# Second layer's first block in seven products, and a token job in every tick

## The chip, the core and the metric

The kernel runs on one core of one Trainium2 chip. The time is device microseconds of a run, first to last instruction with what the launch adds; smaller is better. TensorE is called PE below, VectorE DVE, ScalarE ACT, GpSimd POOL, and SyncE, which issues the DMAs, SP.

## The reference

An attention over 4 batches of 8 heads, with 512 local and 32 global positions of 64 columns, gives 4 x 544 = 2176 tokens of 512 columns. Two gated layers follow; their shapes are 512 x 1536 for gate and value and 1536 x 512 for the output:

```python
def _moe_ref(x, w_gate, w_val, w_out, rms_g):
    xn = x / np.sqrt(np.mean(x * x, -1, keepdims=True) + 1e-06) * rms_g
    g = xn @ w_gate
    silu = g * (1.0 / (1.0 + np.exp(-g)))
    val = xn @ w_val
    return silu * val @ w_out

def _moe2_ref(x, w_gate, w_val, w_out):
    gate = 1.0 / (1.0 + np.exp(-(x @ w_gate)))
    val = x @ w_val
    return gate * val @ w_out
```

The second layer reads the first layer's output. Weights and tokens come as numbers wider than 16 bits and the result is held close to fp32, so that each is split into a high and a low fp16 part, and a product of two such is three matmuls (high by high, low by high, high by low).

## The kernel before

The two layers are cut into twelve blocks of 256 hidden columns, 0 to 5 of the first layer and 6 to 11 of the second. The tokens lie as columns in three parts q = 0, 1, 2 of 768, 768 and 640 tokens; `HN[q]` is half of a part: 384, 384, 320 columns. (6,0) below is block 6 on part 0.

**Products.** Blocks 0 to 2 and, before the change, block 6 (`GP = 6`) are multiplied in the plain way. Block 6 does it in `plain_gv` (L462): for each of two row halves of the weights, two halves of the part, and gate and value, 12 matmuls into one PSUM bank: 96 matmuls of `HN[q]` columns for a part. The other blocks use `quad_gv`: gate and value are each a 2 x 2 by 2 x 2 block product, done with seven products for eight; a product (`prod`, L364) is 6 matmuls, so 84 matmuls for a part. It needs sums of the weights' four pieces and sums of the tokens' four pieces. Its products go to PSUM in four pairs for the gate and four for the value, the first pair holding only one product; the pool `pp` has four buffers of one pair each, used in turn and shared with the output products. ACT copies the first product out (`sa`, L428); DVE adds the other pairs into the tiles G and V (L421: four adds for each, of 2, 2, 1 and 2 products). Then ACT applies the gate (L407), DVE multiplies (L397), ACT writes the high fp16 part `h` (L398) and POOL the low one (L401).

**Weights.** `w_block(g)` queues the steps that convert a block's three matrices, `w_step` takes one off. A conversion is ACT's L139 on each half of the raw words, DVE's L151 and L154 (step 1) and L157 (step 2). For gate and value of a block in seven products come sums: POOL L249 and L250, then DVE L254 and L255; ACT writes high parts (L187) and DVE low parts (L190), of the four pieces (128x1024) and of the three sums (128x768). A plain block has no sums. `w_need(g, 0)` in front of a block runs all steps that are still missing.

**Token sums.** When a part of the first layer's output `yacc[q]` is done, `y_combos(q)` queues jobs that write its fp16 parts `xhi` (ACT L627) and `xlo` (DVE or POOL L630) and then the sums: L590 in place on `yacc` (two on DVE, one on POOL, for each `kt`), then the parts `tt` of the sums (ACT L596, POOL L599). `quad_gv` reads `tt` and three of the four quarters of a part's `xhi` and `xlo`; `plain_gv` reads all four quarters and no `tt`. `j_need(q, i)` runs the jobs of a part that are still missing; before a plain block only those of `xhi` and `xlo`.

**Order.** All of it is written out by hand: every product and output piece calls `tick`, and a tick takes a token job every `pace[2]` ticks and a weight step every `pace[1]`. Engines run their instructions in that order. `GROUPS` pairs blocks for the output products: (4,0), (4,1), (5,0), (4,2), (5,1), (5,2), then (6,0), (6,1), (7,0), (6,2), (7,1), (7,2). The outputs of a part (`out1`, L499, of the first layer; `out2`, L521, of the second; eviction L481 on DVE or L479 on ACT) are issued behind the next block's products: those of part 0 of blocks 4 and 5 behind (4,2), of part 1 behind (5,2), of part 2 behind (6,0).

Of the kernel before, what the change touches and what calls it, by code (L numbers as in the profile page):

```python
# [12 lines left out]
AF = mybir.ActivationFunctionType  # L13
ALU = mybir.AluOpType
# [5 lines left out]
def tile_attention_moe_moe(  # L20
# [17 lines left out]
    nc = tc.nc  # L38
# [33 lines left out]
    xhi = [res.tile([128, 4, 128 * n], F16, tag=f"xhi{i}", name=f"xhi{i}") for i, n in enumerate(PT)]  # L72
    xlo = [res.tile([128, 4, 128 * n], F16, tag=f"xlo{i}", name=f"xlo{i}") for i, n in enumerate(PT)]
# [15 lines left out]

    GS = 3  # L90

    GP = 6
    raw_t = []

    w_pos = [0, 0]
# [35 lines left out]
    def w_scale(n):  # L131

        if n >= NPC or not wide:
            return
        words = w_words.setdefault(n, [])
        if len(words) < 2:
            f = f_tile(n)[:, len(words)]
            words.append(raw_t.pop(0))
            nc.scalar.activation(out=f, in_=words[-1][:, :, 1].bitcast(F32), func=AF.Copy, scale=2.0 ** -112)  # L139
# [57 lines left out]
    def w_block(g):  # L197
# [7 lines left out]
        def small(f):  # L205

            def f2():
                f()
                w_step()
            return f2  # L210
# [5 lines left out]
        def conv(w):  # L216
            n = 3 * g + w
            if g < GS:
                return [lambda: (late(), w_half(n, 0)), lambda: w_half(n, 1)]
            return [lambda: (late(), w_conv1(n)), lambda: w_conv2(n)]  # L220
# [17 lines left out]
        else:  # L238
# [21 lines left out]
            def lo(w, i):  # L260
                a, b = (0, 4)[i], (4, 7)[i]
                w_lo(box[w][i], w_t[g][0][:, w, 0, a:b], w_t[g][0][:, w, 1, a:b])
                if i == 0:
                    w_f.pop(3 * g + w)

            for w in range(2):
                jobs += conv(w)
                if g == GP:
                    def parts(w=w):
                        return [w_t[g][0][:, w, a, 0:4].rearrange("p (j a) f -> p j (a f)", j=2) for a in range(2)]  # L270
                    jobs.append(plain(w, parts))
                else:
                    jobs += [lambda w=w: sums(w), lambda w=w: (sums2(w), hi(w, 0)), lambda w=w: (lo(w, 0), hi(w, 1)),
                             lambda w=w: (lo(w, 1), w_scale(3 * g + w + 1))]
            if g == GP:
                jobs.append(small(late))
# [17 lines left out]
    def w_need(g, i):  # L294
        while not w_done[g][i]:
            w_step()
# [248 lines left out]
    def j_need(q, i):  # L545
        while any(x[0] == q and x[1] <= i for x, _ in jobs):
            jobs.pop(0)[1]()
# [32 lines left out]
    EG = [nc.vector if c == "d" else nc.gpsimd for c in "ddpppppdpd"]  # L580

    def combos(q, kt, b):


        def f(i):
            x = b()

            o, i0, i1 = ((x[:, 0], x[:, :, 1], x[:, 0]), (x[:, 1, 1], x[:, 1, 1], x[:, 0, 0]),
                         (x[:, 1, 0], x[:, 1, 0], x[:, 1, 1]))[i]
            EG[i].tensor_tensor(out=o, in0=i0, in1=i1, op=ALU.subtract)  # L590

        def part(a):
            return tt_t[q][:, a, :, kt].rearrange("p (u v) n -> p u v n", u=2)

        def f2(u):
            nc.scalar.activation(out=part(0)[:, u], in_=b()[:, u], func=AF.Copy)  # L596

        def f3(u):
            EG[4 + u].tensor_tensor(out=part(1)[:, u], in0=b()[:, u], in1=part(0)[:, u], op=ALU.subtract)  # L599
        jobs.extend(((q, 1), x) for x in (lambda: f(0), lambda: (f(1), f2(0)), lambda: (f(2), f3(0)),  # L600
                                     lambda: f2(1), lambda: f3(1)))

    def tt_alloc(q):
        tt_t[q] = pb[1].tile([128, 2, 4, 2, HN[q]], F16, tag=f"tt{q}", name=f"tt{q}")
# [17 lines left out]
    def y_combos(q):  # L622
        n = HN[q]
        yd = yacc[q].rearrange("p (d n) -> p d n", d=4)

        def f(k):
            nc.scalar.activation(out=xhi[q][:, k], in_=yd[:, k], func=AF.Copy)  # L627

        def f2(k):
            EG[8 + k % 2].tensor_tensor(out=xlo[q][:, k], in0=yd[:, k], in1=xhi[q][:, k], op=ALU.subtract)  # L630

        jobs.append(((q, 0), lambda: (tt_alloc(q) if q not in tt_t else None, f(0))))
        jobs.extend(((q, 0), lambda k=k: (f(k), f2(k - 1))) for k in range(1, 4))
        jobs.append(((q, 0), lambda: f2(3)))
        for kt in range(2):
            combos(q, kt, lambda kt=kt: yd[:, kt:4:2].rearrange("p u (t n) -> p u t n", t=2))
# [470 lines left out]
    pace = [0, 2, 2]  # L1107
# [22 lines left out]
    with tc.manual_schedule():  # L1130
# [33 lines left out]
        def flush():  # L1164

            while pend:
                g, key = pend.pop(0)
                if g == group[g][-1]:
                    outs(g, key)
                if 0 < g < GS and key in (2, chunks_b[-1], last.get(g)):  # L1170
                    w_block(g + 2)
                    pace[1] = [2, 4, 3, 3, 4, 4, 4, 2, 4, 2, 2, 2][g]
                if g == NBLK - 1:
                    if isinstance(key, int):
                        y_combos(key)
                    elif key[1] > 0:
                        y_combos(key[0])
# [29 lines left out]
        st_ps.close()  # L1207
        pb["ps"] = st_ps.enter_context(tc.tile_pool(name="pp", bufs=4, space=PSUM, reuse_waits="tile"))
        pb[2] = st_p2.enter_context(tc.tile_pool(name="pb2", bufs=1, reuse_waits="tile"))
        pace[2] = 3  # L1210
        for gr in GROUPS[GS:]:
            a, b = gr[0], gr[-1]
            for g, q in [(a, q) for q in range(3)] if a == b else [(a, 0), (a, 1), (b, 0), (a, 2), (b, 1), (b, 2)]:
                w_need(g, 0)
                j_need(q, 0 if g == GP else 1)
                (plain_gv if g == GP else quad_gv)(g, q, flush)
                if q == 2 and g + 2 < 2 * NBLK:
# [39 lines left out]
```

## Time and profile before

| | |
|---|---|
| median of 3 runs | 938.59 us (936.45 to 938.75) |
| profiled execution, its own time | 939.76 us |
| its span | 938.0 us |
| PE busy | 884.8 us, 94% |
| DVE busy | 666.7 us, 71% |
| ACT, POOL busy | 368.6 and 345.6 us |
| mean granted clock of PE | 0.975 |

The span is cut by the page into 40 slices with the busy share of each engine and PE's granted clock in tenths. The chain of waits follows the work back from the last instruction and names what each step stood behind. Timelines list an engine's instructions in order, equal neighbours merged, with the idle time before them and what ended it. A matmul's row is longer than its turn on PE, since matmuls overlap: the turn is the distance between starts.

### The profile page before, as it was taken

The page shows a single profiled execution, that of the slowest core. Times are in us where ns is not written, and L with a number is a line of the kernel's source. Part 1 is how long each engine was busy: PE and PEld are TensorE (multiplying, and loading weights), DVE is VectorE, ACT ScalarE, POOL GpSimd, SP SyncE. Part 2 cuts the span into 40 slices and gives each one's busy share as a digit, 9 for nine tenths or more (in the row PEclk, how much of TensorE's full clock was granted, in tenths as well). Part 3 has the DMA queues.
Part 4 walks back from the last instruction along what each step waited for, and adds up shares of the span by engine and source line. Part 5 has one row for each costly group of instructions (what it writes and reads, how often), then busy time and mean ns, then how long its engine had stood idle before and what let it go on. Part 6 is the DMA issues. An engine that isn't in the chain of part 4 may idle for free.

```text
span 938.0 us, 19228 instructions
## 1 busy us (share of the span) xinstructions
PE 884.8 (94%) x8119; PEld 551.6 (59%) x8119; DVE 666.7 (71%) x935; ACT 368.6 (39%) x685; POOL 345.6 (37%) x396
## 2 busy tenths in 40 slices
PE   7667889999996999999999799999999999999998
PEld 4455556666674666666666466656556655556553
DVE  3887786646468687899966967737598557997352
ACT  3665565445353343333333344433344213333120
POOL 5548656564354772222221263242221303022120
PEclk9789899999999999999999899999999999999999
DMA  9764452210012111121201121101122011200102
GB/s 194 179 141 102 91 140 53 55 26 2 5 42 95 45 45 46 46 90 45 74 19 45 45 89 46 45 1 46 45 90 90 1 45 45 90 23 1 68 23 101
DMA packets 88999, 58.13 MB, mean 62 GB/s; under 512 B 58448, under 2 KB 83536, under 8 KB 88912
## 3 DMA queue, kind: packets, MB, share of 16 engines
q1 hardware_dynamic: 88912, 56.90, 21.9%
q8 instruction: 64, 1.05, 0.5%
q14 instruction: 23, 0.19, 0.1%
HBM read 52.17 MB, written 4.46 MB: 60 GB/s over the span
## 4 chain that ended last, share of the span: by engine, by line
PE 77%; DVE 14%; issue 3%; ACT 2%; DMA 2%; POOL 1%; SPq 0%; DVEq 0%; ACTq 0%; POOLq 0%
PE p L364 28%; PE p L521 13%; PE b L311 11%; PE p L499 7%; PE b L499 6%; PE p L462 5%; PE b L740 3%; DVE wf L154 2%; DVE wf L157 2%; DVE wf L151 2%; PE b L864 1%; PE b L809 1%; DVE x L854 1%; DVE G L421 1%; DVE wc L190 1%
## 5 line engine op out<-in xcount | busy, mean ns | idle before, releaser
L364 PEld LDWEIGHTS <-wc 128*128 128x128 f16 x2016 | 198.2, 98 | 122.3 <-DVE G L421 4.8
L364 PE MATMUL p<-tt,wc 128*128 128x384 f16 (+1 forms) x1152 | 202.4, 319 | 5.9 <-DVE G L421 5.4
L401 POOL TENSOR_TENSOR h<-V,h 128x768 f16<-128x768 f32 (+1 forms) x48 | 80.8, 1704 | 236.0 <-ACT h L398 218.8
L364 PE MATMUL p<-xhi,wc 128*128 128x384 f16 (+1 forms) x576 | 157.0, 318 | 0.5 <-DVE ya L481 0.5
L311 PE MATMUL b<-xhi,wgv 128*128 128x384 f16 (+1 forms) x576 | 144.0, 320 | 0.0
L521 PE MATMUL p<-wo,h 128*128 128x512 f16 x612 | 133.4, 379 | 0.0
L499 PEld LDWEIGHTS <-wo 128*128 128x128 f16 x864 | 84.7, 99 | 57.1 <-issue 10.2
L311 PEld LDWEIGHTS <-wgv 128*128 128x128 f16 x864 | 83.2, 98 | 47.2 <-issue 3.4
L521 PEld LDWEIGHTS <-h 128*128 128x128 f16 x612 | 59.9, 98 | 71.0 <-POOL h L401 0.2
L311 PE MATMUL b<-xlo,wgv 128*128 128x384 f16 (+1 forms) x288 | 92.1, 320 | 1.3 <-DVE xlo L914 1.3
L364 PE MATMUL p<-xlo,wc 128*128 128x384 f16 (+1 forms) x288 | 91.6, 318 | 0.0
L481 DVE SCALAR_TENSOR_TENSOR ya<-p,ya 128x768 f32<-128x768 f32 (+3 forms) x42 | 42.3, 1016 | 62.1 <-PE p L521 48.2
L697 POOL COPY vw<-vt 32x520 f32<-32x520 f32 (+1 forms) x92 | 80.9, 880 | 12.0 <-DMA vt<-in_v_l_dram 7.8
L499 PE MATMUL b<-hhi,wo 128*128 128x384 f16 (+1 forms) x288 | 73.4, 322 | 8.1 <-ACT hhi L342 7.4
L428 ACT ACTIVATE sa<-p 128x384 f32<-128x384 f32 (+1 forms) x48 | 22.5, 469 | 133.6 <-PE p L364 120.8
L343 POOL TENSOR_TENSOR hlo<-t,hhi 128x384 f16<-128x384 f32 (+1 forms) x36 | 38.4, 1066 | 90.5 <-ACT hhi L342 90.4
L398 ACT ACTIVATE h<-V 128x1536 f16<-128x1536 f32 (+1 forms) x24 | 33.9, 1413 | 95.2 <-DVE V L397 95.2
L499 PE MATMUL p<-h,wo 128*128 128x384 f16 (+1 forms) x432 | 67.3, 317 | 0.0
L421 DVE TENSOR_TENSOR V<-p,V 128x768 f32<-128x768 f32 (+3 forms) x72 | 56.6, 786 | 12.4 <-PE p L364 9.6
L421 DVE TENSOR_TENSOR G<-p,G 128x768 f32<-128x768 f32 (+3 forms) x72 | 56.5, 785 | 8.4 <-PE p L364 5.9
L154 DVE SCALAR_TENSOR_TENSOR wf<-raw,wf 128x512 int32<-128x512 int32 x72 | 55.8, 806 | 1.6
L157 DVE SCALAR_TENSOR_TENSOR wf<-raw,wf 128x512 int32<-128x512 int32 x72 | 53.9, 778 | 0.6
(137 smaller groups left out, 1320.4 us busy)
## 6 DMA issues: line engine op xcount, KB each, us to landing
raw<-in_moe_w_gate_dram SPq DMA_DIRECT2D x24, 512.0 KB, 3.7
raw<-in_moe_w_val_dram SPq DMA_DIRECT2D x24, 512.0 KB, 4.4
raw<-in_moe_w_out_dram SPq DMA_DIRECT2D x24, 512.0 KB, 3.9
k<-in_k_l_dram SPq DMA_DIRECT2D x16, 256.0 KB, 4.0
q<-in_q_l_dram SPq DMA_DIRECT2D x16, 256.0 KB, 4.2
vt<-in_v_l_dram SPq DMA_DIRECT2D x32, 128.0 KB, 4.8
out_dram<-ya SPq DMA_DIRECT2D x16, 256.0 KB, 2.2
vg<-in_v_g_dram SPq DMA_DIRECT2D x16, 64.0 KB, 3.7
```

The lines of the kernel that those rows point to most:

```text
L154: nc.vector.scalar_tensor_tensor(out=u[:, j], in0=w_words[n][j][:, :, 1], scalar=-0x80000000, in1=u[:, j], op0=ALU.bitwise_and, op1=ALU.bi ...
L157: nc.vector.scalar_tensor_tensor(out=u[:, j], in0=w_words[n][j][:, :, 0], scalar=29, in1=u[:, j], op0=ALU.logical_shift_right, op1=ALU.bit ...
L311: nc.tensor.matmul(p[:, 0:n], wgv[:, j, gv, a, k * 128:(k + 1) * 128], x[xi][:, k, o:o + n], start=(i == 0), stop=(i == 11),)
L343: EH[3].tensor_tensor(out=lo, in0=t, in1=hi, op=ALU.subtract)
L364: nc.tensor.matmul(p, wc[:, w, a, wi, kt * 128:(kt + 1) * 128], r, start=(i == 0), stop=(i == 5))
L401: EH[j // 2].tensor_tensor(out=lo[:, i:i + 2], in0=vj[:, i - j:i - j + 2], in1=hi[:, i:i + 2], op=ALU.subtract)
L421: nc.vector.tensor_tensor(out=o, in0=p, in1=i, op=ALU.add)
L462: nc.tensor.matmul(gv[:, w], wc[:, w, a, c, (k % 2) * 128:(k % 2 + 1) * 128], x[q][:, k, h * n:(h + 1) * n], start=(i == 0), stop=(i == 11))
L481: nc.vector.scalar_tensor_tensor(out=ya, in0=p, scalar=1.0 / WS, in1=ya, op0=ALU.mult, op1=ALU.add)
L499: nc.tensor.matmul(p[:, i, 0:n], wo[:, j, a, d * 128:(d + 1) * 128], hh[:, j, ho:ho + n], start=(c == 0), stop=(c == 6 * len(gr) - 1),)
L521: nc.tensor.matmul(p[:, i], hh[:, j, (i0 + i) * 128:(i0 + i + 1) * 128], wo[:, j, a, :], start=(c == 0 and g == gr[0]), stop=(c == 5 and g ...
L697: eng.tensor_copy(out=dst, in_=src)
```

## The change

`GP` becomes `None`: no block is plain any more, so block 6 goes through `quad_gv`, its weight steps get the sums, and `j_need` asks for its token sums too. `pace[2]` becomes 1: after the first layer's plain blocks a token job is taken in every tick instead of every third. `y_combos` writes only the first half of quarters k = 0 and 1 of `xhi` and `xlo`; the second half of those is read by no product of seven.

```diff
-    GP = 6
+    GP = None
...
+        m = [n, n, 2 * n, 2 * n]
+
         def f(k):
-            nc.scalar.activation(out=xhi[q][:, k], in_=yd[:, k], func=AF.Copy)
+            nc.scalar.activation(out=xhi[q][:, k, 0:m[k]], in_=yd[:, k, 0:m[k]], func=AF.Copy)
 
         def f2(k):
-            EG[8 + k % 2].tensor_tensor(out=xlo[q][:, k], in0=yd[:, k], in1=xhi[q][:, k], op=ALU.subtract)
+            EG[8 + k % 2].tensor_tensor(out=xlo[q][:, k, 0:m[k]], in0=yd[:, k, 0:m[k]], in1=xhi[q][:, k, 0:m[k]],
+                                        op=ALU.subtract)
...
-        pace[2] = 3
+        pace[2] = 1
```

Lines behind L626 stand up to four lines later in the changed kernel (`xlo` is L630 before and L633 after).

DVE's instructions at the change from (5,1) to (5,2): in the first row V and G are multiplied for (5,1), L421 adds for (5,2), L590 are token sums of part 0, L157 and L190 convert weights.

```order
 L397 SCALAR_TENSOR_TENSOR V<-V,G 128x1536
 L421 TENSOR_TENSOR G<-p,sa 128x2x320
-L590 TENSOR_TENSOR ya_79<-ya_79 128x768
-L157 SCALAR_TENSOR_TENSOR wf<-raw,wf 128x512 x2
+L190 SCALAR_TENSOR_TENSOR wc<-wf,wc 128x1024
 L421 TENSOR_TENSOR G<-p,G 128x2x320
 L421 TENSOR_TENSOR G<-p,G 128x320
-L590 TENSOR_TENSOR ya_79<-ya_79 128x384
-L421 TENSOR_TENSOR G<-p,G 128x2x320
+L421 TENSOR_TENSOR G<-p,G 128x2x320
+L190 SCALAR_TENSOR_TENSOR wc<-sm,wc 128x768
```

The token sums and the conversion's second step have left this place (they stand in (5,1), ahead of it, or behind the products); a low part of block 6's weights stands there instead.

DVE's instructions before, where (6,1) ends and (7,0) begins (rows with L471 and L473 are the plain block's gate times value and its low part; the last row is the first add of (7,0)):

```order
L190 SCALAR_TENSOR_TENSOR wc<-wf,wc 128x1024
L471 SCALAR_TENSOR_TENSOR G<-p,G 128x384
L473 TENSOR_TENSOR h_7357<-G,h_7356 128x384
L190 SCALAR_TENSOR_TENSOR wc<-sm,wc 128x768
L471 SCALAR_TENSOR_TENSOR V<-p,V 128x384
L473 TENSOR_TENSOR h_7357<-V,h_7356 128x384
L151 TENSOR_SCALAR wf<-wf 128x1024
L154 SCALAR_TENSOR_TENSOR wf<-raw,wf 128x512 x2
L590 TENSOR_TENSOR ya_80<-ya_80 128x768
L157 SCALAR_TENSOR_TENSOR wf<-raw,wf 128x512 x2
L421 TENSOR_TENSOR G<-p,sa 128x768
```

The same place now; the first row is the last add of (6,1), the last the first add of (7,0):

```order
L421 TENSOR_TENSOR V<-p,V 128x768
L254 TENSOR_TENSOR sm<-wf 128x256
L255 TENSOR_TENSOR sm<-wf,sm 128x256
L190 SCALAR_TENSOR_TENSOR wc<-wf,wc 128x1024
L190 SCALAR_TENSOR_TENSOR wc<-sm,wc 128x768
L151 TENSOR_SCALAR wf<-wf 128x1024
L154 SCALAR_TENSOR_TENSOR wf<-raw,wf 128x512 x2
L397 SCALAR_TENSOR_TENSOR V<-V,G 128x1536
L157 SCALAR_TENSOR_TENSOR wf<-raw,wf 128x512 x2
L421 TENSOR_TENSOR G<-p,sa 128x768
```

Between the last add of one block and the first of the next there are now eight rows in one piece, the steps that `w_need(7, 0)` ran at once among them.

POOL's instructions from the start of (6,0) until block 7's gate sums, now:

```order
L633 TENSOR_TENSOR xlo_77<-ya_80,xhi_74 128x384
L633 TENSOR_TENSOR xlo_77<-ya_80,xhi_74 128x768
L590 TENSOR_TENSOR ya_80<-ya_80 128x384
L599 TENSOR_TENSOR tt_4738<-ya_80,tt_4738 128x2x384 x2
L590 TENSOR_TENSOR ya_80<-ya_80 128x384
L599 TENSOR_TENSOR tt_4738<-ya_80,tt_4738 128x2x384
L401 TENSOR_TENSOR h_7084<-V,h_7083 128x768 x2
L599 TENSOR_TENSOR tt_4738<-ya_80,tt_4738 128x2x384
L249 TENSOR_TENSOR sm<-wf 128x256
L250 TENSOR_TENSOR wf<-wf 128x256
```

Before, only the two L630 rows of part 1, one late L599 of part 0 and the sums L249 and L250 stood in this stretch; the four L599 of part 1 stood in (6,1) and (7,0), and there was no L401 of block 6.

## Rows read from the trace of the kernel before

**Rows 1.** Waits of PE from 360 us on: total us, times, longest.

```profile
PE p L364 <- DVE G L421: 5.4, 3, 4.4
```

**Rows 2.** PE's timeline, (5,2) and the outputs behind it: start, us, instruction [idle before].

```profile
521.55 0.97 PE L364 MATMUL p<-tt,wc 128*128 128x320 f16 x6 [0.59 <-DVE G L421]
...
527.77 3.38 PE L364 MATMUL p<-tt,wc 128*128 128x320 f16 x12 [4.43 <-DVE G L421]
...
533.68 15.76 PE L499 MATMUL p<-h,wo 128*128 128x384 f16 x96
```

**Rows 3.** DVE's timeline around that wait.

```profile
521.42 0.95 DVE L590 TENSOR_TENSOR ya<-ya 128x768 f32<-128x768 f32 x1
522.28 4.17 DVE L157 SCALAR_TENSOR_TENSOR wf<-raw,wf 128x512 int32<-128x512 int32 x2
526.38 1.33 DVE L421 TENSOR_TENSOR G<-p,G 128x640 f32<-128x640 f32 x2
527.63 0.55 DVE L590 TENSOR_TENSOR ya<-ya 128x384 f32<-128x384 f32 x1
528.10 0.82 DVE L421 TENSOR_TENSOR G<-p,G 128x640 f32<-128x640 f32 x1
...
529.56 2.38 DVE L190 SCALAR_TENSOR_TENSOR wc<-wf,wc 128x1024 f16<-128x1024 f32 x1
```

**Rows 4.** POOL's timeline there.

```profile
522.14 3.77 POOL L401 TENSOR_TENSOR h<-V,h 128x768 f16<-128x768 f32 x2 [8.84 <-ACT h L398]
...
529.22 1.65 POOL L599 TENSOR_TENSOR tt<-ya,tt 128x768 f16<-128x768 f32 x1
```

**Rows 5.** Stretches: us; busy (count) PE, PEld, DVE, ACT, POOL; PE's clock; DMA.

```profile
501.70:538.80 37.10, 32.08 (x195) 19.86 (x194) 34.10 (x41) 15.86 (x20) 10.09 (x6) 0.91 0.17 57
549.30:607.20 57.90, 57.90 (x374) 36.41 (x373) 44.11 (x60) 26.56 (x41) 19.80 (x15) 1.00 0.17 55
```

**Rows 6.** Two earlier idle times of PE in its timeline.

```profile
288.63 0.32 PE L499 MATMUL b<-hhi,wo 128*128 128x384 f16 x1 [3.06 <-ACT hhi L342]
...
304.18 0.27 PE L499 MATMUL b<-hhi,wo 128*128 128x256 f16 x1 [4.31 <-ACT hhi L342]
```

**Rows 7.** Stretches, columns as above: PE's clock behind each of three idle times.

```profile
290.00:292.00 2.00, 2.00 (x14) 1.21 (x13) 2.00 (x2) 1.20 (x3) 2.00 (x2) 1.00 0.25 87
...
306.00:308.00 2.00, 2.00 (x11) 1.40 (x10) 0.58 (x2) 1.12 (x2) 2.00 (x2) 0.52 0.00 0
...
528.00:530.00 2.00, 2.00 (x9) 1.18 (x8) 2.00 (x4) 1.76 (x3) 1.74 (x2) 0.50 0.70 228
```

**Rows 8.** Chain of waits in order of time: start, us, engine, line, count.

```profile
570.28 23.40 PE p L462 x144
593.68 13.65 PE p L364 x84
```

**Rows 9.** DVE's timeline in an earlier block in seven products.

```profile
454.22 0.41 DVE L254 TENSOR_TENSOR sm<-wf 128x256 f32<-128x256 f32 x1
...
455.01 0.95 DVE L421 TENSOR_TENSOR G<-p,G 128x768 f32<-128x768 f32 x1
455.88 1.22 DVE L190 SCALAR_TENSOR_TENSOR wc<-wf,wc 128x1024 f16<-128x1024 f32 x1
457.01 0.95 DVE L421 TENSOR_TENSOR V<-p,sa 128x768 f32<-128x768 f32 x1
...
461.42 0.68 DVE L151 TENSOR_SCALAR wf<-wf 128x1024 int32<-128x1024 int32 x1
462.13 1.29 DVE L154 SCALAR_TENSOR_TENSOR wf<-raw,wf 128x512 int32<-128x512 int32 x2
463.35 1.75 DVE L397 SCALAR_TENSOR_TENSOR V<-V,G 128x1536 f32<-128x1536 f32 x1
465.01 1.30 DVE L157 SCALAR_TENSOR_TENSOR wf<-raw,wf 128x512 int32<-128x512 int32 x2
466.22 0.96 DVE L421 TENSOR_TENSOR G<-p,sa 128x768 f32<-128x768 f32 x1
```

## The prediction

> **What bounds the kernel now.** I first read PE's waits behind the attention [rows 1]: the reader is to see that from 360 us on PE waits almost only for DVE's adds into G, 5.4 us in three times, 4.4 of them in one. So in this half PE sets the time, and DVE decides where PE stands still. PE's timeline puts the long wait into (5,2), right ahead of the changed block [rows 2]: 0.59 and 4.43 us, and then 24 matmuls of 320 columns that take from 527.77 to 533.68. The stretches show why: at 528 to 530 us the granted clock is 0.50, the lower level (1.2 GHz) [rows 7]. DVE is busy for 34.10 of 37.10 us there, but for 44.11 of 57.90 in (6,0) to (7,0), where PE never waits [rows 5].
>
> DVE's and POOL's timelines, laid side by side, give the price that matters [rows 3, 4]. The two L157 need 1.2 us elsewhere (465.01 to 466.22 [rows 9]); at 522.28, while POOL runs two L401 from 522.14 to 525.91, they take 4.17. L190 at 529.56 takes 2.38 for 1.22, beside L599. The adds L421 at 526.38 and 528.10, whose one input is in PSUM, keep their time. DVE thus lost 3.0 + 1.2 = about 4.1 us to 10.09 us of POOL work [rows 5], a share of 0.41. I call this the lock.
>
> **Step 1, the products.** Plain: 144 matmuls of 384 columns in 23.40 us, so 15.60 for 96; in sevens 84 take 13.65 [rows 8]. Two parts save 1.95 each, the part of 320 columns 1.63 by its columns: 5.5 us off PE, which is full there.
>
> **Step 2, (5,1) and (5,2).** The order shows block 6's conversions thinned out (its sums come in between) and part 0's token sums pulled ahead of them. DVE's work from 501.70 to the third add of (5,2)'s G, by distances between starts [rows 3, 9]: conversion 1.93 and 1.21, `xlo` 0.47 + 0.86, the adds of (5,1) 6.5 (0.87 for two products, 1.25 x 384/320 = 1.5 for two and one; both twice, for G and V, with another 0.87), token sums 2 x (0.86 + 0.47), L254 and L255 0.79, L397 1.66, first add of (5,2) 0.73 by its columns, low part 1.13, adds 1.25: 19.2 us. POOL's work beside it, 1.65 us per 768 columns [rows 4], is 5504 columns, 11.8 us; at 0.41 the lock costs 4.8. The add ends at 525.7. PE would want it at 527.77 - 4.43 - 0.59 = 522.7, so it waits 3.0 us for 5.0, in pieces, since the adds are late one by one. An idle time of 3.06 us left the clock at 1.00, those of 4.31 and 4.43 were followed by 0.52 and 0.50 [rows 6, 7, 2]; so the fall goes too. It cost 5.9 us for matmuls of 3.25 (24 x 13.65/84 x 320/384): 2.7. Step 2 gains 5.0 - 3.0 + 2.7 = 4.7, call it 4.8 with the half quarters of `xlo`. Without any lock it would be 7.7, with twice the lock a loss of 2.6 (7.6 us of waits, and the clock falls).
>
> **Step 3, (6,0) to (7,0).** Here the plain block's cover goes. PE from the start of (6,0) to where it needs the first add of (7,0): 14 products 13.65, outputs of part 2 13.0 (96 x 0.1355), 14 products 13.65, then eight of (7,0) 7.8, since four PSUM pairs let PE run ahead of an add by five products: 48.1 us. DVE has to do until that add ends: adds 6.5 + 6.5 + 0.87 = 13.9; five L481 3.8; part 1's and 2's `xlo` and token sums 4.0 + 3.4; two L397 3.3; and for the weights four conversions of 3.14, three low parts of 1.13 and three of 0.86, sums 2 x 0.79, 20.2: together 48.6. That alone is PE's whole time, and POOL's work comes on top: `xlo`, L590, L599, L401 and two pairs of sums, 11072 columns, 23.8 us, at 0.41 a lock of 9.8. Before, most of it had 14 us of free DVE time beside it [rows 5]. DVE also waits for POOL, for L250 behind two L401 and an L599, about 1 us. 48.6 + 9.8 + 1 - 48.1 = 11.3 us of waits of PE. Bounds: no more lock than the 4.1 us measured gives 4.6 (no wait for POOL); a share of 0.6, 15.8. I take 0.41, measured where DVE was as full.
>
> The Trainium skill, page "SBUF — State Buffer", section "Who interferes with whom", says that a DVE instruction with two SBUF inputs and a GpSimd instruction that reads SBUF exclude each other for whole instructions, and that one with a single SBUF input is free. The trace agrees in L157's 4.17 us and the adds' unchanged time. By that rule POOL's 23.8 us lie free only beside the 17.7 us of adds and evictions, so the lock is at least 6.1, the waits at least 7.6 and the time at least 938.6; by the rows it is what follows.
>
> **Step 4, the clock there.** The waits grow toward (7,0): between the last add of (6,1) and the first of (7,0) stand L254, L255, two L190, a conversion and L397, 8 us of DVE work in one piece, where PE's lead is five products, 4.9 us, and is already used up. So I expect a last wait of over 4 us and a fall of the clock like that at 528 us: 2.7.
>
> **What costs nothing.** ACT's halved L627 and its table load, which moves from L470 to L407, lie on an engine that DVE does not wait for there. The sums' ACT work goes behind POOL's. SP's DMAs stand as before. The new wait of DVE in (5,1), L254 for L250, holds one add, which PE wants 4 us later; uncovered it costs 1. `j_need` finds its jobs done. Behind (7,0) the conversions shift by a row or two, where waits of 0.4 to 0.5 us are all there is: plus or minus 1.
>
> **The sum.** The profiled execution took 939.76, 1.2 over the median; the differences belong to either, and I put them on the median: 938.6 - 5.5 - 4.8 + 11.3 + 2.7 = 942.3.
>
> **Rivals.** First: the same waits, but in pieces too short for the clock to fall: 939.6. For it, 3.06 us left the clock up; against it, the eight rows in one piece. Second, faster: DVE keeps up. Mechanism: POOL's work meets DVE's gaps and adds, not its two-input work, in (6,0) and (6,1), so that the lock stays at 4.1 and the first add of (7,0) ends within 53 us of the start of (6,0). Waits 4.6, no fall: 938.6 - 5.5 - 4.8 + 4.6 = 932.9. For it: from 549 to 607 us POOL worked 19.80 us without a wait of PE; against it: DVE was then busy for three quarters and would now be full. Third, worse: POOL's and DVE's instructions alternate and each holds the other, share 0.6: waits 15.8, time 946.8. For it: L157's second instruction stood behind a second L401.
>
> **How the numbers follow.** Forecast 0.42, no fall 0.20, DVE keeps up 0.22, worse 0.16. The forecast alone is 939.5 to 945 (step 2's waits 2 us either way, the lock 1 to 2). 0.3% is 2.8 us and about what a measurement of this kernel tells from no change: faster means below 935.8, slower above 941.4. The forecast falls slower with 0.25 and same with 0.17; no fall gives same 0.15, faster 0.03, slower 0.02; the second rival faster 0.18, same 0.04; the third is slower. Together faster 0.21, same 0.36, slower 0.43. Leaving out a tenth at each end, from the second rival's lower half and the third's upper, the range is 932.3 to 947.
>
> **What would show it.** Step 1: no L462 and 84 matmuls of (6,0) in 13.7 us where it doesn't wait. Step 2: the waits in (5,2) under 4 us, clock 1.00 in the 20 us behind, and the outputs of part 1 starting near 529 for 533.7. Step 3: PE's waits for L421 from (6,0) to (7,0) of 9 to 13 us, the longest at (7,0); DVE full there, with L157, L190, L397 and `xlo` above their usual time. Step 4: a stretch at 0.5 behind it. If those waits are under 6 us, step 3 is wrong and the lock is not additive; if the waits in (5,2) are as long as before, step 2 is.

## The result and the profile after

The changed kernel took 948.04 us (median of 4 runs, 946.88 to 948.44), the kernel before, run beside it, 938.67 (936.45 to 938.98). The ratio is 1.0108, 95% interval 1.0096 to 1.0120. The change costs 9.4 us. The forecast was 942.3 with a range up to 947.0: the direction was right, the loss more than twice what the sum gave, and the time lies above the range.

The waits of PE behind the attention, of after; the columns are those of [rows 1]:

```profile
PE p L364 <- DVE V L421: 8.8, 5, 2.5
PE p L364 <- DVE G L421: 6.5, 5, 4.7
PE p L364 <- POOL tt L599: 3.0, 1, 3.0
PE p L364 <- ACT sa L428: 1.1, 1, 1.1
PE p L364 <- DVE ya L481: 0.5, 1, 0.5
```

The reader is to see two things: the waits of 5.4 us in three times have become 19.9 in 13, and two of them are not for DVE: a short one for ACT, and one of 3.0 us for POOL, which no step of the prediction had. The timeline of PE tells where they lie, first those of (5,1) and (5,2), which answer to [rows 2]:

```profile
516.21 1.80 PE L364 MATMUL p<-tt,wc 128*128 128x320 f16 x12 [1.43 <-DVE V L421]
520.01 0.30 PE L364 MATMUL p<-xhi,wc 128*128 128x320 f16 x1 [2.00 <-DVE V L421]
523.22 0.97 PE L364 MATMUL p<-tt,wc 128*128 128x320 f16 x6 [0.60 <-DVE G L421]
525.61 1.80 PE L364 MATMUL p<-tt,wc 128*128 128x320 f16 x12 [0.61 <-DVE G L421]
528.88 15.76 PE L499 MATMUL p<-h,wo 128*128 128x384 f16 x96
```

and then the two longest ones from (6,0) to (7,0):

```profile
576.65 0.80 PE L364 MATMUL p<-tt,wc 128*128 128x384 f16 x2 [2.95 <-POOL tt L599]
...
609.14 2.08 PE L364 MATMUL p<-tt,wc 128*128 128x384 f16 x6 [4.74 <-DVE G L421]
```

With 0.22, 2.24, 2.48 and 1.12 us beside them they make 13.75 us. The clock behind both, in the stretches of after, columns as in [rows 7]:

```profile
576.00:578.00 2.00, 1.35 (x5) 0.66 (x5) 0.00 (x0) 0.00 (x0) 1.92 (x3) 0.53 0.03 8
578.00:580.00 2.00, 2.00 (x10) 0.94 (x9) 1.85 (x4) 1.89 (x3) 0.08 (x1) 0.62 0.00 0
...
608.00:610.00 2.00, 0.85 (x3) 0.41 (x3) 1.90 (x3) 2.00 (x3) 1.39 (x1) 0.50 0.49 138
610.00:612.00 2.00, 2.00 (x8) 0.93 (x7) 1.86 (x4) 0.56 (x2) 1.86 (x2) 0.50 1.05 369
```

The spans of the two profiled executions differ by 8.6 us (946.6 and 938.0), and the starts of (5,1), (6,0) and (7,1) in PE's timelines, first of before, then of after, divide this into pieces:

```profile
500.63 0.33 PE L364 MATMUL p<-xhi,wc 128*128 128x384 f16 x1
549.28 0.33 PE L462 MATMUL p<-xhi,wc 128*128 128x384 f16 x1
635.75 0.33 PE L364 MATMUL p<-xhi,wc 128*128 128x384 f16 x1
...
498.52 0.33 PE L364 MATMUL p<-xhi,wc 128*128 128x384 f16 x1
544.48 0.33 PE L364 MATMUL p<-xhi,wc 128*128 128x384 f16 x1
644.15 0.33 PE L364 MATMUL p<-xhi,wc 128*128 128x384 f16 x1
```

Up to the start of (5,1), 498.52 for 500.63, the two kernels issue the same work; the 2.1 us belong to the executions (in the eleven traces here with the same work up to that point it starts between 496.85 and 500.63). From there to the outputs of part 1 (called the first stretch from here on) it is 30.36 us for 33.05, a gain of 2.7. From the start of (6,0) to that of (7,1) (the second stretch) it is 99.67 for 86.47, a loss of 13.2. The outputs between the two take the same time in both, and behind (7,1) the difference is 0.2. So the whole loss lies in the second stretch, and there the products save their 5.5 us while PE stands still for 13.75 and loses about 5.0 more, most of it by being slowed twice.

What DVE did in that stretch, its timeline of after, eight pieces of it:

```profile
548.36 2.73 DVE L157 SCALAR_TENSOR_TENSOR wf<-raw,wf 128x512 int32<-128x512 int32 x2
...
559.23 3.45 DVE L590 TENSOR_TENSOR ya<-ya 128x768 f32<-128x768 f32 x2
...
564.06 1.85 DVE L151 TENSOR_SCALAR wf<-wf 128x1024 int32<-128x1024 int32 x1
...
578.12 0.42 DVE L254 TENSOR_TENSOR sm<-wf 128x256 f32<-128x256 f32 x1 [4.74 <-POOL wf L250]
...
589.00 3.57 DVE L154 SCALAR_TENSOR_TENSOR wf<-raw,wf 128x512 int32<-128x512 int32 x2
...
594.62 1.95 DVE L157 SCALAR_TENSOR_TENSOR wf<-raw,wf 128x512 int32<-128x512 int32 x2
...
599.35 1.61 DVE L254 TENSOR_TENSOR sm<-wf 128x256 f32<-128x256 f32 x1 [0.26 <-POOL wf L250]
...
608.14 0.95 DVE L421 TENSOR_TENSOR G<-p,sa 128x768 f32<-128x768 f32 x1
```

and POOL's timeline beside its idle time:

```profile
571.57 3.44 POOL L401 TENSOR_TENSOR h<-V,h 128x768 f16<-128x768 f32 x2 [6.20 <-ACT h L398]
574.97 1.63 POOL L599 TENSOR_TENSOR tt<-ya,tt 128x768 f16<-128x768 f32 x1
576.56 0.71 POOL L249 TENSOR_TENSOR sm<-wf 128x256 f32<-128x256 f32 x1
577.36 0.72 POOL L250 TENSOR_TENSOR wf<-wf 128x256 f32<-128x256 f32 x1
```

Two L401, an L599 and the weights' first sums stand on POOL in one row. PE waits for the L599 until 576.6, DVE for the L250 until 578.1, with an L481 and all that follows queued behind it. The first add of (7,0) starts at 608.14, the eight rows ahead of it come in one piece from 599.35, as the order had shown.

### The profile page after: what moved, and what is told of

The parts are those of the page before. It is cut to its first block, busy times and chain, and to the rows that moved or that the text cites. A ratio compares the mean times of both kernels' runs of the same rounds, so it can differ in the third digit from the quotient of the medians.

```text
span 946.6 us, 19184 instructions
## 1 busy us (share of the span) xinstructions
PE 882.5 (93%) x8083; PEld 546.5 (58%) x8083; DVE 684.4 (72%) x944; ACT 368.4 (39%) x675; POOL 355.4 (38%) x406
## 4 chain that ended last, share of the span: by engine, by line
PE 72%; DVE 18%; issue 3%; ACT 2%; POOL 2%; DMA 1%; SPq 1%; DVEq 0%; ACTq 0%; POOLq 0%
PE p L364 30%; PE p L521 14%; PE b L311 11%; PE b L499 6%; PE p L499 6%; DVE wf L154 3%; PE b L744 2%; DVE wf L151 2%; DVE wf L157 2%; DVE G L421 1%; PE b L868 1%; DVE ya L590 1%; DVE x L858 1%; POOL vw L701 1%; DVE V L421 1%
## 5 line engine op out<-in xcount | busy, mean ns | idle before, releaser
L364 PEld LDWEIGHTS <-wc 128*128 128x128 f16 x2268 | 222.4, 98 | 153.4 <-issue 21.7
L364 PE MATMUL p<-tt,wc 128*128 128x384 f16 (+1 forms) x1296 | 227.6, 319 | 16.3 <-DVE V L421 6.8
L401 POOL TENSOR_TENSOR h<-V,h 128x768 f16<-128x768 f32 (+1 forms) x54 | 90.0, 1687 | 259.1 <-ACT h L398 224.8
L364 PE MATMUL p<-xhi,wc 128*128 128x384 f16 (+1 forms) x648 | 177.3, 320 | 3.6 <-DVE V L421 2.0
L364 PE MATMUL p<-xlo,wc 128*128 128x384 f16 (+1 forms) x324 | 103.6, 320 | 0.0
L701 POOL COPY vw<-vt 32x520 f32<-32x520 f32 (+1 forms) x92 | 80.7, 878 | 12.5 <-DMA vt<-in_v_l_dram 8.3
L481 DVE SCALAR_TENSOR_TENSOR ya<-p,ya 128x768 f32<-128x768 f32 (+3 forms) x42 | 42.2, 1017 | 58.7 <-PE p L521 46.7
L398 ACT ACTIVATE h<-V 128x1536 f16<-128x1536 f32 (+1 forms) x27 | 38.1, 1413 | 105.6 <-DVE V L397 105.6
L428 ACT ACTIVATE sa<-p 128x384 f32<-128x384 f32 (+1 forms) x54 | 25.2, 468 | 134.5 <-PE p L364 121.7
L421 DVE TENSOR_TENSOR V<-p,V 128x640 f32<-128x640 f32 (+2 forms) x81 | 63.7, 786 | 14.9 <-PE p L364 12.2
L421 DVE TENSOR_TENSOR G<-p,G 128x640 f32<-128x640 f32 (+2 forms) x81 | 63.6, 786 | 8.4 <-PE p L364 5.6
L154 DVE SCALAR_TENSOR_TENSOR wf<-raw,wf 128x512 int32<-128x512 int32 x72 | 58.1, 838 | 1.6
L157 DVE SCALAR_TENSOR_TENSOR wf<-raw,wf 128x512 int32<-128x512 int32 x72 | 55.1, 796 | 0.6
```

The lines of the kernel that those rows point to most:

```text
L154: nc.vector.scalar_tensor_tensor(out=u[:, j], in0=w_words[n][j][:, :, 1], scalar=-0x80000000, in1=u[:, j], op0=ALU.bitwise_and, op1=ALU.bi ...
L157: nc.vector.scalar_tensor_tensor(out=u[:, j], in0=w_words[n][j][:, :, 0], scalar=29, in1=u[:, j], op0=ALU.logical_shift_right, op1=ALU.bit ...
L364: nc.tensor.matmul(p, wc[:, w, a, wi, kt * 128:(kt + 1) * 128], r, start=(i == 0), stop=(i == 5))
L398: nc.scalar.activation(out=hi[:, j:e], in_=vj, func=AF.Copy)
L401: EH[j // 2].tensor_tensor(out=lo[:, i:i + 2], in0=vj[:, i - j:i - j + 2], in1=hi[:, i:i + 2], op=ALU.subtract)
L421: nc.vector.tensor_tensor(out=o, in0=p, in1=i, op=ALU.add)
```

## The experiments

Each was timed beside the kernel before (medians 936.93 to 937.71 us), and is a variant of after unless it says before. A ratio is to the kernel before. After itself stands at 1.0108. In after the first stretch takes 30.36 us and the second 99.67, in before 33.05 and 86.47.

**What of the change costs it.** First the job in every tick alone, in before:

```diff
-        pace[2] = 3
+        pace[2] = 1
```

> The kernel before with one change: a token job in every tick; block 6 stays plain, with all quarters written. Theory 'sum': POOL and DVE have room beside the plain block, so nothing waits in (6,0) to (7,0); in (5,1) and (5,2) DVE's order changes and the wait of 5.0 us and the clock's fall may move by 2 either way. Time 936 to 941, PE's waits in (6,0) to (7,0) under 2 us. Theory 'pace': 943 to 948, with most of the waits of the changed kernel.

943.38 us, ratio 1.0065 (1.0051 to 1.0079). The pace alone costs some 6 us, without a product less: this is the time of the pace theory, not the 936 to 941 of the sum theory, which took DVE and POOL to have room beside the plain block. In the traced execution (946.58 us) the second stretch takes 93.04 us and the first 34.32. PE's waits from 470 to 700 us:

```profile
PE p L364 <- DVE G L421: 4.2, 3, 2.1
PE p L364 <- DVE V L421: 4.1, 2, 3.1
PE p L364 <- DVE V L471: 1.5, 2, 1.2
PE p L364 <- DVE G L471: 0.6, 1, 0.6
```

In the last two, products of (7,0) wait for PSUM pairs that the plain block's own L471 have not freed yet: with the jobs of parts 1 and 2 taken in every tick even that block's cover is used up. But with seven products the slower pace is worse:

```diff
-        pace[2] = 1
+        pace[2] = 3
```

> Seven products in block 6 and the halves stay; a token job is taken in every third tick again, as before. Theory 'sum': part 2's token sums (DVE 3.4 us, POOL 7 us) leave the stretch up to the first add of (7,0) and part 0's leave (5,1), so PE's waits in (6,0) to (7,0) fall from 13.8 to 7 to 9 us, while jobs left over are run at once before (6,0) and (6,1), which costs 1 to 2. Time 941 to 944, still not under the kernel before. Theory 'pace' (the job in every tick is the loss, and seven products alone gain their 5.5 us): 931 to 934. Theory 'place': the late L599 is gone, the piece before (7,0) stays: 943.

956.70 us, ratio 1.0215 (1.0200 to 1.0231), which no theory had. In PE's waits 12.5 us are for L596 and 9.3 for L599: what is left of a part's token sums is then issued in one go right in front of the products that read them. On the other hand (5,1) and (5,2) have no wait there. The sums have to be made somewhere, and the pace only says who waits for them. The third part of the change, the halves:

```diff
-        m = [n, n, 2 * n, 2 * n]
+        m = [2 * n] * 4
```

> After, with whole quarters of the tokens' high and low parts again, also the four halves that no product reads. Adds to DVE and POOL one half quarter of a low part per part each (about 0.5 us on DVE, 0.8 on POOL, three times) and the same to ACT. Sum theory: 1.5 + 0.41 x 2.4 = 2.5 us more DVE time, of which what lies in the full stretches shows: plus 1.5 to 3, so 949.5 to 951. Rival (this part of the change does nothing): 947 to 948.5.

949.55 us, ratio 1.0127 (1.0111 to 1.0143): about 1.8 us more than after by the ratios, but the intervals overlap; leaving the halves out is worth something between nothing and some 4 us.

**Place or sum.** Two runs change only where things stand: the last L599 of part 1 ahead of (6,0)'s product of gate and value, and the weights' steps spread.

```diff
+        if (g, q) == (NBLK, 0):
+            j_need(q + 1, 1)
         if not pend or pend[0][0] != group[pend[0][0]][-1]:
```

> Only the place of one POOL instruction changes: the last L599 of part 1's token sums is issued before the multiplication of (6,0), so that it stands ahead of the two L401 on POOL and not behind them. Theory 'sum' (DVE's work from (6,0) to (7,0), its lock with POOL and its wait for L250 set when the first add of (7,0) ends; PE's waits only share that out): PE's wait of 2.95 us for L599 in (6,1) goes, but the waits behind it grow by nearly as much, since DVE still waits 4.7 us for L250 and does the same work. Only a fall of the clock, about 2 us, may go. Time 945 to 948. Theory 'place' (the loss is in two places, PE's wait for the late L599 and the eight rows in one piece before (7,0)): the wait of 2.95 and the clock's fall behind it go, 5 us, time 943.

948.07 us, ratio 1.0117 (1.0101 to 1.0133): no change, where the place theory had 943. The wait for L599 is gone, in its place PE waits 0.67 for V, 1.44 for L483 (L481 in after) and 1.31 for G, and the wait at (7,0) is 4.74 us as in after; the second stretch takes 99.57. Then:

```diff
-                    pace[1] = [2, 4, 3, 3, 4, 4, 4, 2, 4, 2, 2, 2][g]
+                    pace[1] = [2, 4, 3, 3, 4, 3, 4, 2, 4, 2, 2, 2][g]
```

> After, with block 7's weight steps every three ticks from (6,0) on instead of every four: the eight rows of DVE that stood right ahead of (7,0) are spread over (6,1) and (6,2). DVE's and POOL's work up to the first add of (7,0) is the same in sum, and a little more of the weight work lies ahead of it. Sum theory (DVE's work, lock and its waits for POOL set it): waits of PE from (6,0) to (7,0) move and stay at 13 to 15 us, 947 to 950. Rival, the clock and the piece (one idle time of PE over 4 us, and the falls behind it, are the loss): the last wait under 3 us, both falls gone, 943 to 944.

951.61 us, ratio 1.0149 (1.0135 to 1.0163). The eight rows are spread, the wait at (7,0) is 3.48 us, and one of 6.67 for L481 stands in (6,1). Both runs speak against the place: the wait comes up elsewhere. They fit a sum of work, but the second was worse than the sum theory allowed (950).

**The clock.** Products are repeated into the PSUM pair that they have just filled, two in (6,1) and four in (7,0), where PE is about to stand still:

```diff
-            nc.scalar.activation(out=a, in_=prods((0, (0, 0)))[:, 0], func=AF.Copy)
+            p0 = prods((0, (0, 0)))
+            for _ in range({(6, 1, 0): 2, (7, 0, 1): 4}.get((g, q, w), 0)):
+                prod(p0[:, 0], g, q, w, 0, (0, 0), False)
+            nc.scalar.activation(out=a, in_=p0[:, 0], func=AF.Copy)
```

> After, with products repeated into the PSUM pair that they have just filled, where PE is about to stand still: twice in (6,1) ahead of the wait for L599, four times in (7,0) ahead of the wait of 4.74 us. TensorE gets 6 x 0.975 = 5.9 us of work more, most of it inside 7.7 us of idle time. What it tells is whether the two clock falls behind those waits cost time of their own. Theory that they cost 5.0 us (12.0 us of PE work at about 0.55 to 0.6): no fall behind either, 943 to 944.5. Rival (the adds set the time there whatever PE's clock is): falls gone or not, 946.5 to 948.5. Rival (the repeats delay the adds and the waits behind them grow): 950 or more.

946.39 us, ratio 1.0091 (1.0073 to 1.0108). The row of PE's timeline that answers to 609.14 of after:

```profile
609.04 1.14 PE L364 MATMUL p<-tt,wc 128*128 128x384 f16 x6 [0.42 <-DVE G L422]
```

The idle time of 4.74 us is filled and the clock behind it is 1.00, but the add comes at the same microsecond, although the fall at 576 is gone too. What that fall had cost has become a wait of 1.27 us for G at 586.10, and another fall has come, at 600, which moves the add as little. Up to (7,0) the end is DVE's, and a slow PE there costs nothing. Only the fall behind the last wait has a price: the second stretch takes 97.5 us for 99.7, 2.2 us. My expectation of 5.0 was wrong by the first fall, and the time lies at the lower edge of the rival by which the adds set it; the estimate of 2.7 for one fall was near. By the ratios the gain is 1.6 us, with intervals that overlap after's, so it rests on the two traces.

**DVE's wait for POOL.** The weights' first sums of blocks 6 and 7 go to DVE, so that L254 waits for no one:

```diff
+                e = [nc.vector] * 2 if g in (6, 7) else ES
-                ES[0].tensor_tensor(out=sm[:, 0], in0=x[:, 0], in1=x[:, 2], op=ALU.subtract)
-                ES[1].tensor_tensor(out=x[:, 2], in0=x[:, 2], in1=x[:, 3], op=ALU.add)
+                e[0].tensor_tensor(out=sm[:, 0], in0=x[:, 0], in1=x[:, 2], op=ALU.subtract)
+                e[1].tensor_tensor(out=x[:, 2], in0=x[:, 2], in1=x[:, 3], op=ALU.add)
```

> After, with L249 and L250 (the weights' first sums) of blocks 6 and 7 on DVE instead of POOL, so that L254 waits for no other engine. In the trace of after DVE stood idle for L250 for 4.74 us from 573.4 and for 0.26 us at 599.35, since L249 and L250 stood on POOL behind two L401 and an L599. From (6,0) to (7,0) DVE loses those 5.0 us of waiting, gets four sums of 0.42 (1.7 us), and the lock gives back 0.41 x 2.9 = 1.2. If DVE's wait for POOL is the term that was mis-sized in my sum, that is 4.5 us off: 942.5 to 944.5. Rival (PE's own wait of 2.95 us for L599, behind the same two L401, sets that place whatever DVE does): 946 to 948. Rival (without a wait DVE only reaches the next instruction that waits for POOL or ACT): 945 to 946.

946.63 us, ratio 1.0106 (1.0090 to 1.0123), by the ratio the time of after; only the rival of PE's own wait for L599 had a time like this. DVE's timeline where it had stood idle (here L250, L251 and L255 are after's L249, L250 and L254):

```profile
572.55 1.13 DVE L250 TENSOR_TENSOR sm<-wf 128x256 f32<-128x256 f32 x1
573.71 1.74 DVE L251 TENSOR_TENSOR wf<-wf 128x256 f32<-128x256 f32 x1
575.38 0.81 DVE L482 SCALAR_TENSOR_TENSOR ya<-p,ya 128x640 f32<-128x640 f32 x1
576.11 1.12 DVE L255 TENSOR_TENSOR sm<-wf 128x256 f32<-128x256 f32 x1
...
606.57 0.95 DVE L422 TENSOR_TENSOR G<-p,sa 128x768 f32<-128x768 f32 x1
```

The wait is gone, and the same sums that take 0.42 to 0.46 us at 597.7 take 1.13, 1.74 and 1.12 beside the two L401 and the L599 (POOL 571.56 to 576.96). The first add of (7,0) comes 1.6 us earlier, not 4.5. PE's wait for the L599 stays, 3.3 us. So most of the wait came back as lock: while POOL works off its row, DVE's two-input work hardly gets on. The unchanged time is a balance, though. The second stretch takes 97.57 us, 2.1 less than in after, and the first 32.03, 1.7 more, since block 6's sums went to DVE as well, into (5,1), where the clock fell to 0.59 at 522 us.

**POOL's share.** The low parts of the second layer's token sums are left out (ACT writes the high part a second time in their place), and then, in another run, made by DVE instead of POOL:

```diff
-            EG[4 + u].tensor_tensor(out=part(1)[:, u], in0=b()[:, u], in1=part(0)[:, u], op=ALU.subtract)
+            if low:
+                EG[4 + u].tensor_tensor(out=part(1)[:, u], in0=b()[:, u], in1=part(0)[:, u], op=ALU.subtract)
+            else:
+                nc.scalar.activation(out=part(1)[:, u], in_=b()[:, u], func=AF.Copy)
```

> The changed kernel, but the low fp16 parts of the second layer's token sums are left out: ACT copies the sums there a second time where POOL subtracted (12 L599, 19 us of POOL work, 10.9 of it between (6,0) and the first add of (7,0)). DVE's work is the same. Theory 'sum' with the lock: DVE loses 0.4 of 10.9, 4.5 us, less to POOL, waits 1.6 us less for L250, and PE's wait for L599 goes; clock falls with it. PE's waits in (6,0) to (7,0) fall from 13.8 to 5 to 7 us; time 936 to 940. Without a lock (DVE's own work is the bound): only the wait for L599 with its clock fall goes, 5 us: 943.

```diff
+            e = nc.vector if second else EG[4 + u]
-            EG[4 + u].tensor_tensor(out=part(1)[:, u], in0=b()[:, u], in1=part(0)[:, u], op=ALU.subtract)
+            e.tensor_tensor(out=part(1)[:, u], in0=b()[:, u], in1=part(0)[:, u], op=ALU.subtract)
```

> After, with the second layer's twelve L599 (low parts of the tokens' sums) on DVE instead of POOL in each pass over the tokens. In block 6's stretch POOL loses 21.3 us of work, DVE gets twelve instructions of 0.86 or 0.73 us, 9.8 in all. Sum theory (each us of POOL beside a full DVE costs DVE 0.41): +9.8 - 8.7 by the lock, DVE's wait for L250 down from 4.74 by the L599's 1.6, PE's wait for L599 of 2.95 gone or turned into one for DVE: minus 0.5 to minus 3.5, 944.5 to 947.5. Rival without a lock: +9.8 - 4.6 = +5, 952 to 954. Rival (POOL's queue, in which L250 and L599 stand behind the two L401, is the loss): 942 to 943.5.

Left out: 934.89 us, ratio 0.9976 (0.9968 to 0.9985), 12 to 13 us less than after and a little more than the sum theory gave (936 to 940). Its first stretch takes 26.01 us, its second 90.66. On DVE: 948.40, ratio 1.0109 (1.0093 to 1.0125), the time of after, one microsecond above the range of the sum theory and far from both rivals. DVE's groups from 498 to 610 us, of after (busy us, mean ns, idle before):

```profile
L590 DVE TENSOR_TENSOR ya<-ya 128x768 f32<-128x768 f32 (+3 forms) x12 | 12.8, 1065 | 0.3
L154 DVE SCALAR_TENSOR_TENSOR wf<-raw,wf 128x512 int32<-128x512 int32 x12 | 10.0, 878 | 0.2
L151 DVE TENSOR_SCALAR wf<-wf 128x1024 int32<-128x1024 int32 x6 | 5.3, 883 | 0.0
L254 DVE TENSOR_TENSOR sm<-wf 128x256 f32<-128x256 f32 x4 | 3.7, 915 | 7.5 <-POOL wf L250 7.5
```

and with the low parts on DVE:

```profile
L600 DVE TENSOR_TENSOR tt<-ya,tt 128x768 f16<-128x768 f32 (+1 forms) x12 | 11.3, 945 | 3.5 <-ACT tt L596 3.5
L590 DVE TENSOR_TENSOR ya<-ya 128x768 f32<-128x768 f32 (+3 forms) x12 | 8.6, 720 | 0.3
L154 DVE SCALAR_TENSOR_TENSOR wf<-raw,wf 128x512 int32<-128x512 int32 x12 | 7.8, 688 | 0.2
L151 DVE TENSOR_SCALAR wf<-wf 128x1024 int32<-128x1024 int32 x6 | 4.1, 684 | 0.0
L254 DVE TENSOR_TENSOR sm<-wf 128x256 f32<-128x256 f32 x4 | 1.7, 420 | 4.3 <-POOL wf L250 4.3
```

The same instructions of the same shape are shorter as soon as POOL has 21.3 us less to do. With L255 (3.0 and 1.7), L397 (7.1 and 6.8) and L157, which grows (9.8 and 11.3), DVE gets 9.7 us back, 0.46 us per us of POOL; the prediction had 0.41. With 3.2 us less waiting for L250 that is 12.9, and the twelve L600 cost 11.3 and 3.5 of waiting for ACT. Beside a full DVE a piece of POOL's work thus costs about what it would cost on DVE.

**More room.** Before the change as after it, DVE is busy for about 16 of the 30 us from 470 to 500, under the outputs of part 0. The weights of blocks 6 and 7 are released ahead of the outputs of parts 0 and 1 instead of behind them, first in after, then in before:

```diff
+                def fl(g=g, q=q):
+                    if q == 2 and g + 2 < 2 * NBLK:
+                        w_block(g + 2)
+                        pace[1] = [2, 4, 3, 3, 4, 4, 4, 2, 4, 2, 2, 2][g]
+                    flush()
+                e = g in (4, 5)
-                (plain_gv if g == GP else quad_gv)(g, q, flush)
-                if q == 2 and g + 2 < 2 * NBLK:
+                (plain_gv if g == GP else quad_gv)(g, q, fl if e else flush)
+                if q == 2 and g + 2 < 2 * NBLK and not e:
```

> After, with block 6's and block 7's weight work released ahead of the outputs of part 0 and part 1 of the pair before, instead of behind them (the buffers are free by then). The trace of after shows DVE busy for 8.6 of 20 us from 480 to 500, under the outputs of part 0, and 90 per cent from 500 to 608. Some 5.3 us of DVE work (two conversions, L254, L255, one L190) and 1.4 us of POOL work move into that free time. Sum theory: the waits of (5,1) and (5,2), 4.6 us, nearly go, and what is left of the gain comes off the waits from (6,0) on, since block 7's steps also start earlier: 5.3 + 0.6 = 5.9, with a clock fall less 8: 940 to 942.5. Rival (only what stands right ahead of (7,0) counts): waits of (5,1) and (5,2) go, those from (6,0) on stay at 13 to 14, 943.5 to 945. Rival (a full DVE is not the cause): no change, 947 to 949.

> Before, with the same edit: the weight work of blocks 6 and 7 released ahead of the outputs. Its waits in (5,1) and (5,2), 5.0 us with a clock fall of 2.7, are the only ones near. Sum theory: both go, 931 to 933, and the plain block's 24 us pieces hide the rest; the distance to the seven-product kernel with the same edit stays 7 to 11 us. Rival (the weights were what made seven products slower): the distance falls under 4 us.

After: 944.32 us, ratio 1.0072 (1.0059 to 1.0084). The time is that of the rival by which only what stands ahead of (7,0) counts, but by luck, since no account had where it came from. Two of the accounts had the waits of (5,1) and (5,2) go; they grew from 4.6 to 6.5 us, with the clock at 0.50 at 524, and the first stretch takes 33.66 us, 3.3 more than in after: two L154 take 4.07 us there and two L157 3.90, beside POOL's L599. The second takes 92.11, 7.6 less, with 7.3 us of waits. Before: 931.13, ratio 0.9936 (0.9924 to 0.9949), faster than both kernels. Here all the gain lies in the first stretch, 26.90 us for 33.05; the second keeps its 86.47. All that its PE waits for from 360 us on:

```profile
PE p L364 <- DVE G L421: 1.9, 3, 1.2
PE p L364 <- DVE V L421: 0.7, 1, 0.7
PE p L364 <- DVE ya L481: 0.5, 1, 0.5
```

The distance between the two is 13.2 us, more than the 7 to 11 expected: the room helps the plain block more than the seven products, since it covers nearly all that the plain block left open. Once more with seven products, the weights' steps every two and three ticks instead of four:

```diff
-                        pace[1] = [2, 4, 3, 3, 4, 4, 4, 2, 4, 2, 2, 2][g]
+                        pace[1] = [2, 4, 3, 3, 2, 3, 4, 2, 4, 2, 2, 2][g]
```

> After, with the weights released ahead of the outputs as in the run before this, and steps every two ticks (block 6's) and three (block 7's) instead of every four. Another six us or so of DVE work (L254, L255, two L190, a conversion) goes from (5,1) and (5,2) into the outputs of part 0, where DVE still had 9 of 30 us free, and block 7's move forward as well. Sum theory: off the 944.3 of the slower pace come 4 to 6 us, 938.5 to 940.5; still not below the kernel before with the same edit (931.1), since all free time is then used up to (6,0). Rival (an order in which the weights run in front of the tokens' jobs only moves the waits, as one tick less did from (6,0) on): 943 to 946.

941.37 us, ratio 1.0037 (1.0026 to 1.0049), 3 us off the slower pace; the sum theory had 938.5 to 940.5, the rival 943 to 946. PE still waits 13.8 us from 470 to 700, 4.3 of them in one piece at 517, and DVE is busy for 40.06 of the 44 us from 500 to 544. The second stretch is down to 88.13 us, 1.7 more than with the plain block; the loss now stands in the first, 34.45. No version with seven products in that block that makes all of the sums came under the kernel before.

## Why the prediction was too low

**Step 1** held: no L462 is left, and the 84 matmuls of (7,1), where PE does not wait, take 13.65 us (644.15 to 657.80); those of (6,0) take 14.4 with 0.22 of waiting and some smaller gaps. **Step 2** had the right sign and the clock: no fall, and the outputs of part 1 start at 528.88 for the 529 expected, though 2.1 us of that were there before (5,1) began. Measured from there the gain is 2.7, not 4.8, and it is nearly all the clock's: the waits came to 4.64 us instead of 3.0, for 5.0 before, and are over the 4 that the prediction had set as its sign. Up to the third add of (5,2)'s G six instructions are lengthened, `xlo` (2.01 us for 0.47), two L590 (3.78 for 1.5), L254 (1.20 for 0.42), L255 (1.75 for 0.42) and L397 (2.15 for 1.75), by 6.3 us in all against a lock of 4.8, and POOL worked 14.3 us there, not 11.8.

**Step 3** is the step that failed, by its size. It put the end of the first add of (7,0) 59.4 us behind the start of (6,0): 48.6 of work, 9.8 of lock, 1 of waiting for POOL. It came after 64.6, and the stretch of the trace between the two (columns as in [rows 7]) says in which term:

```profile
544.48:609.09 64.61, 50.89 (x314) 30.65 (x312) 58.41 (x66) 27.96 (x38) 29.39 (x22) 0.96 0.16 50
```

DVE was busy for 58.41 us, which is what the sum had for work and lock together, 58.4. It was idle for 6.2 instead of 1: 5.0 for L250 and 1.2 in short gaps. The lengthened rows of the timeline, L157 at 548.36 and 594.62, L590 at 559.23, L151 at 564.06, L154 at 589.00 and L254 at 599.35, add up to about 8.7 of lock for the 9.8 expected, so that the work was about 1 us more. The term that was mis-sized is the waiting for POOL. The order showed the L250 behind two L401 and an L599, and the prediction named it; I took one microsecond for it without adding up the row that stands ahead: 3.44 + 1.63 + 0.71 + 0.72 = 6.5 us of POOL from the moment at which ACT delivers h, against a DVE that had only two L481 and 1.8 us in all left to do. That the same row holds up PE itself, through the last L599, the prediction did not have at all. The run with the sums on DVE shows that sizing the wait alone would not have told what its removal is worth: without it the add comes 1.6 us earlier, since the lock takes its place. The signs that the prediction had set for this step came: 9.7 us of waits for L421, the longest at (7,0). So the mechanism was right, a full DVE held up by POOL, and the size of one term wrong.

**Step 4** expected one fall of the clock for 2.7 us and got two. The second is no miss in time: the run with filled waits shows that the fall at 576 is hidden behind DVE, and the one at (7,0) costs 2.2. In the terms of the sum step 3 came to 64.6 - 48.1 = 16.5 us for 11.3, of which PE shows 13.75 as waits and the rest mostly as slow products behind the first fall.

The sum, with the profiles' pieces: -2.7 in place of -4.8, and from (6,0) to (7,1) +13.2 (-5.5 + 16.5 + 2.2) in place of +8.5 (-5.5 + 11.3 + 2.7), so 6.8 us more loss than forecast, 5.2 of them step 3's and 2.1 step 2's, less 0.5 of step 4's; the executions' 2.1 us ahead of (5,1) hide a part of it in the spans, and in the medians the miss is 5.7.

Of the rivals, that DVE keeps up is refuted by after's own trace, where the first add of (7,0) ended after 64.6 us and not within 53; that the clock does not fall, by the 0.50 at 610. The worse lock gave a near time (946.8) for a wrong reason: it wanted a share of 0.6, and the runs show less. Nor is the share a constant, as the prediction took it: it was 0.46 where POOL's work was taken away, 0.44 up to (5,2)'s third add (6.3 us for 14.3 of POOL) and 0.30 from (6,0) to the first add of (7,0) (8.7 for 29.4). That step 3's lock came near has some luck in it, a smaller share of more POOL time. One reading behind the 0.41 does not carry either: of the two adds said to keep their time beside POOL, the pair at 526.38 ran after POOL's L401 had ended at 525.91; only the one at 528.10 ran beside it. The rule of the Trainium skill (page "SBUF — State Buffer", section "Who interferes with whom") that whoever comes first holds the shared port for whole instructions agrees with the two L154 of 3.57 us for 1.29. The same section of the Trainium skill says that `tensor_scalar` can fall under it too, in modes that use both ports, which the prediction left out; L151 with its one input took 1.85 us for 0.69 beside an L599, which agrees, though no run shows its mode.

What stays open is why the run with block 7's weights spread is 3.6 us slower than after: its traced execution took 949.04 us and does not show the difference, with 99.90 us for the second stretch against 99.67. Open too is why work released early lengthens the first stretch with seven products.

## What to carry to other kernels

A cheaper product pays only if the engine that prepares and collects its operands has room in the same stretch, so add up that engine's work between two fixed points of the bottleneck, with a share of the time of an engine that holds it up (0.30 to 0.46 here, so a range and not a figure), before counting a single saved matmul. Where an instruction waits for another engine's queue, add up the whole row ahead of it from its own releaser; and expect that moving the work off that queue can turn most of the wait into a lock rather than into a gain. When a stretch is full, look for a stretch ahead of it that is not and release work into it, here worth 6 us to the kernel with eight products; then see whether the wait has gone or only moved ahead, as it did with seven.

## What the runs showed of the hardware

The clock did not follow the length of the last idle time alone. An idle time of 3.06 us left it up in the kernel before [rows 6], one of 3.48 did in the run with the weights spread, but 2.95 us in after were followed by 0.53 in the next stretch of 2 us, and 2.21 us in the seven-product run with early weights (at 577.77) by 0.63 and then 0.51. After's wait of 2.48 us at 598 was followed by 1.00; the wait of the same length at the same place in the run with filled waits by 0.50:

```profile
600.00:602.00 2.00, 2.00 (x8) 0.93 (x7) 1.97 (x3) 0.96 (x2) 0.57 (x1) 0.50 0.08 29
```

So the no-fall rival, which rested on 3.06 us, rested on too little.

POOL seems to be held up by DVE as well: an L599 of 768 columns took 2.64 us at 557.31 in after, for 1.65 elsewhere, and DVE's L190, with two inputs, ran from 557.06 to 558.44.
